# Joint first query blocks, four score banks with one visit per pair, an all-fp32r second batch and a lower VectorE bias in a planned attention + gated-MoE kernel

## The chip, the cores and the metric

One core of a Trainium2 chip runs the whole program. The metric is device time in microseconds; three runs of the kernel before gave 697.58, 698.43 and 699.06, median 698.43. Engines are called PE (TensorE matmul), PEld (its weight loads), DVE (VectorE), ACT (ScalarE), POOL (GpSimd) and SP (the queue that issues the DMAs). L443 is line 443 of the kernel.

## The reference: what is computed

```python
batch, n_heads, seq, head_dim = (4, 12, 448, 64)
scores = scale * np.matmul(q, k.transpose(0, 1, 3, 2))
scores = np.where(mask, -1000000000.0, scores)          # causal
scores = scores - np.max(scores, axis=-1, keepdims=True)
attn = np.exp(scores)
attn = attn / (np.sum(attn, axis=-1, keepdims=True) + 1e-09)
attn_out = np.matmul(attn, v)
# heads side by side: 1792 tokens x 768, then the gated feed-forward, d_ff = 1536
g = x @ w_gate
silu = g * (1.0 / (1.0 + np.exp(-g)))
out = silu * (x @ w_val) @ w_out
```

All of it is float32, causal attention over 4 batches of 12 heads, then three matrix products over 1792 tokens.

## The kernel before, in words

**Tiling.** The 448 queries of a batch are one chunk (`CHUNKS`), and the chunk is also the token tile of the feed-forward. Heads are worked in pairs (6 pairs per batch, 24 in all), the even head's operands on partitions 0 to 63 and the odd one's on 64 to 127, so that the two heads' score matmuls stand side by side in the array. Queries are cut at 0, 64, 192, 320, 448: block 0 has 64 queries, the others 128. Block i needs the keys up to its own end, so the scores of one head are 64, 192, 320 and 448 wide.

**Attention, per pair.** Scores (L443) go to PSUM banks `S`; DVE adds the causal mask, takes the row maximum and writes to SBUF (L467, `p`); ACT takes exp with the row sums (L478); DVE makes the reciprocal of the sums (L489, L490); the rows are scaled (norm: L499 on ACT, L503 on POOL, or a DVE form); PE transposes the result into PSUM banks `T` in three groups per head, group 0 shared by the two heads (L548, 4 transposes), groups 1 and 2 of 3 transposes each for either head (L577); the `T` bank is copied out (`ph`, L293); then PE multiplies with V into bank `O` (PV) and the result goes to `xs`.

**Two arithmetics.** `NS` and `NP` say by batch how scores and PV are done. `n` is plain float32 (L443 on `qraw`, `kraw`; L640). `s` splits each operand into two fp32r parts, hi and lo, and makes three fp32r passes for the scores (L443 on `QS`, `KS`) and two for PV (L612 with `ph`, L614 with `pl`; block 0 in one pass, hi and lo stacked). There `ph` is the hi part, made by ACT, and DVE makes the lo part from the same `T` bank (L315), so the bank is free only after both. In batch 0 all six pairs are `n`, in batch 1 the even pairs, in batches 2 and 3 none: 9 pairs `n`, 15 pairs `s`.

**Feed-forward.** Weights come as 36 groups of 128 x 768. In chunk 0 each group is put together from raw 64-bit words (`wide`, `top`, `wraw`), split into hi and lo (`whl`) and stored for the later chunks, which load it. A group needs 18 matmuls of 448 columns (L742 to L744, three fp32r passes, banks `M`): 2592 in all. The planner places them in units of three.

**Order.** Nothing is issued in the order of the code. Each step is an `op` with a due time, dependencies, the buffers it takes and frees, and a cost on each engine that can do it. `Planner.run` gives every engine its list, in which the engines then run strictly; `BIAS` is added to an engine's finishing time when alternatives are compared, `LAT` stands for the time from one engine to another, and `CAPS` says how many buffers a tag has. PSUM has 8 banks: `S` 2, `T` 3, `O` 1, `M` 2. The scores of a pair are two ops: blocks 0 and 3 in one visit of PE, blocks 1 and 2 in another (`SG`), each with one `S` bank per head (in batch 0 the second takes `M`).

Of the kernel before, what the change touches and what calls it, by code (L numbers as in the profile page):

```python
# [8 lines left out]
F32 = mybir.dt.float32  # L9
# [8 lines left out]
P = 128  # L18
D = 64
# [9 lines left out]
UW = 0  # L29
NS = ['n', 'ns', 's', 's']  # L30
NP = ['n', 'ns', 's', 's']
LEN = [46.6, 112.0, 258.9, 133.6, 58.1]
# [17 lines left out]
DLAT = 1.8  # L50
CAPS = {'S': 2, 'T': 3, 'O': 1, 'M': 2, 'qraw': 3, 'kraw': 3, 'vraw': 3, 'QS': 1, 'KS': 1, 'VS': 3, 'ph': 2, 'pl': 2, 'p': 2, 'tmp': 2, 't': 3, 'osb': 2, 'wide': 3, 'wraw': 2, 'whl': 5}

# [168 lines left out]
def kernel(  # L221
# [34 lines left out]
    back, mask = masks[:, : maskX + P], masks[:, P:]  # L256
    sums = [cpool.tile([P, NKC], F32, tag=f"sums{i}", name=f"sums{i}") for i in range(NR)]
    rec = [cpool.tile([P, NKC], F32, tag=f"rec{i}", name=f"rec{i}") for i in range(NR)]
    xs = [cpool.tile([P, T], F32, tag=f"xs{i}", name=f"xs{i}") for i in range(KD)]
# [6 lines left out]
    nc.vector.memset(top, 0)  # L266
    for t_ in sums:
        nc.vector.memset(t_, 1.0)
    make_identity(nc, ident)
    nc.gpsimd.memset(masks, 0.0)  # L270
    for m_, step, base in ((back, 1, 1 - P), (mask, -1, maskX)):
        nc.gpsimd.affine_select(
            out=m_, in_=m_, pattern=[[step, maskX + P]], compare_op=ALU.is_ge,
            fill=BIG, base=base, channel_multiplier=1,
        )

    pl_ = Planner()
# [81 lines left out]
    st = [dict() for _ in range(NU)]  # L359
    loads, scored, parts = {}, {}, {}  # L360
    ptile, pfirst, normed, first0, dues = {}, {}, {}, {}, {}
    xs_ops, xs_res, xlast = {}, {}, {}

    def attention(u):
# [8 lines left out]
        if h % 2 == 0:  # L373
# [24 lines left out]
        if not npv:  # L398
            rV = Res("VS")

            def newv():
# [4 lines left out]
                           lambda: raw(s["VS"])[:, :, 0:D]), due(9), [v1], [], [rV, rv])  # L406

        rsum = Res(f"sums{u % NR}")
        exps, rps = [], {}
        if h % 2 == 0:  # L410
            if not U.ns:
                rQ, rK = Res("QS"), Res("KS")
                sp = []
                for nm, r_, src, ld, rr in (("Q", rQ, "q", lq, rq), ("K", rK, "k", lk, rk)):
                    def newsp(nm=nm):
# [4 lines left out]
                                        lambda nm=nm: raw(s[nm])[:, 0]), due(1), [x1], [], [r_, rr]))  # L420
            for gi_, sess in enumerate(SG):
                stag = "M" if c == 0 and gi_ % 2 else "S"
                rSs = {(y, x): Res(stag) for y in (0, 1) for x in range(len(sess))}

                def score(gi_=gi_, sess=sess, stag=stag):
                    passes = ((None, None),) if U.ns else ((0, 0), (0, 1), (1, 0))
                    for x, blks in enumerate(sess):
                        B_ = [bank(stag, f"S{u + y}_{gi_}_{x}") for y in (0, 1)]
                        off = 0
                        for i in blks:  # L430
                            q0, q1_ = U.qi[i][1]
                            for y in (0, 1):
                                st[u + y][f"S{i}"] = B_[y][:, off : off + q1_]
                            off += q1_
                    for x, blks in enumerate(sess):
                        for i in blks:
                            q0, q1_ = U.qi[i][1]
                            for z, (a, b_) in enumerate(passes):
                                for y in (0, 1):
                                    half = slice(D * y, D * y + D)  # L440
                                    Q = s["qw"][half] if U.ns else s["Q"][half, a]
                                    K = s["kw"][half] if U.ns else s["K"][half, b_]
                                    nc.tensor.matmul(st[u + y][f"S{i}"][: U.rows[i]], Q[:, q0 : q0 + U.rows[i]], K[:, :q1_] if y else K[:, S - q1_ :],  # L443
                                                     start=z == 0, stop=z == len(passes) - 1)
                ws = [U.qi[i][1][1] for blks in sess for i in blks]
                if U.ns:
                    so = op({"PE": (sum(cost("PE", "n", w) + 0.06 for w in ws) + TS, score), "kind": "s"}, due(2), [lq, lk],
                            list(rSs.values()), [rq, rk])
# [7 lines left out]
        for i, (q0, q1_) in U.qi:  # L456
            r = U.rows[i]
            sl = U.pslot(q1_)
            rp = ptile[u, i] if h % 2 else Res(f"p{sl}")
            so, rS = scored[u, i]  # L460

            def rowmax(i=i, q0=q0, q1_=q1_, r=r, sl=sl):
                if h % 2 == 0:
                    s[f"pp{i}"] = st[u + 1][f"pp{i}"] = buf([P, 2 * q1_], F32, f"p{sl}", "p", f"p{u}_{i}")
                p = s[f"p{i}"] = s[f"pp{i}"][:, (h % 2) * q1_ : (h % 2 + 1) * q1_]
                m = s[f"m{i}"] = pool.tile([P, 1], F32, tag=f"m{sl}", name=f"m{u}_{i}", bufs=2 * CAPS["p"])
                nc.vector.tensor_tensor_reduce(  # L467
# [8 lines left out]
            def expo(i=i, r=r):  # L476
                p = s[f"p{i}"]
                nc.scalar.activation(  # L478
                    p[:r], p[:r], AF.Exp, bias=s[f"m{i}"][:r], scale=-1.0,
                    accum_out=sums[u % NR][:r, i : i + 1],  # L480
# [5 lines left out]
        def recip():  # L486
            i0, i1 = U.qi[0][0], U.qi[-1][0] + 1
            sm, rc = sums[u % NR][:, i0:i1], rec[u % NR][:, i0:i1]
# [4 lines left out]
        norms = {}  # L493
        for i, (q0, n) in U.qi:
            r = U.rows[i]

            def na(i=i, r=r):
# [13 lines left out]
            }, due(6), [rc], [], [rps[i], rsum])  # L511

        blocks = parts[u] = {}
        normed[u] = norms
# [23 lines left out]
        if h % 2:  # L538

            rT = Res("T")  # L540
            both_ = [norms[i] for i in norms] + [normed[u - 1][i] for i in norms]

            def transp0():
                pt = s["T0"] = st[u - 1]["T0"] = bank("T", f"T{u}_0")
                for i, (q0, _) in U.qi:
                    r = U.rows[i]
                    w = U.qi[i][1][1]
                    nc.tensor.transpose(pt[:, q0 : q0 + r], s[f"pp{i}"][:r, w - D : w + D], ident[:r, :r])  # L548
            tr = op({"PE": (0.109 * len(U.qi), transp0), "kind": "t"}, due(7), both_, [rT], list(rps.values()))
            if npv:  # L550
                rh = Res("ph0")

                def newp():
                    s["ph0"] = st[u - 1]["ph0"] = buf([P, N], F32, "ph0", "ph", f"ph{u}_0")
                    return s["ph0"]
                hi = op(copies("psum", N, newp, lambda: s["T0"][:, :N], engines="AD"), due(8), [tr], [rh], [rT])
                for y in (0, 1):
# [7 lines left out]
        for g, js in enumerate([[1], [2, 3]], 1):  # L565
            cols = [U.qb - U.base(j) for j in js]
            offs = [sum(cols[:i]) for i in range(len(js))]
            n = sum(cols)
            rT = Res("T")
            todo = [(j, o_, i, e) for j, o_ in zip(js, offs) for i, e in U.qi if e[0] >= U.kb[j][0]]  # L570

            def transp(g=g, todo=todo):
                pt = s[f"T{g}"] = bank("T", f"T{u}_{g}")
                for j, o_, i, (q0, q1_) in todo:
# [21 lines left out]
    def weigh(u):  # L596
# [33 lines left out]
        for j in range(nj):  # L630
# [3 lines left out]
            def pv(g=g, j=j, o_=o_, w=w):  # L634
                if j == 0:
                    st[u0]["O"] = bank("O", f"O{u}")
                for v in (u0, u):
                    half = D * (v - u0)
                    kr = parts[v][j][3]
                    nc.tensor.matmul(st[u0]["O"][half : half + D, U.base(j) - U.qa : N], st[v]["v"][kr, j],  # L640
                                     st[v][f"ph{g}"][kr, o_ : o_ + w], start=(j == 0), stop=(j == nj - 1))
            dur = cost("PE", "n", w) + 0.02
            last = op({"PE": (dur + (TV if j == 0 else 0), pv), "kind": "v"}, due(10), d0 + d1 + [last],
# [240 lines left out]
```

## Time and profile before

| what | value |
|---|---|
| median of 3 runs | 698.43 us (697.58 to 699.06) |
| the profiled execution: its time, its span | 697.08 us, 695.3 us |
| PE busy | 682.3 us, 98% of the span |
| PEld, DVE, ACT, POOL busy | 598.1, 333.8, 346.9, 162.6 us |
| granted clock of PE, whole span | 1.0 of full speed |
| DMA | 165.05 MB, 236 GB/s on HBM over the span |
| PE rows of the feed-forward (L742 to L744) | 2592 |

A matmul's row is longer than its turn: matmuls are pipelined, and the next starts before the row ends. What a matmul costs is therefore read from starts: within a stream of M matmuls they are 0.20 us apart. "A visit" below is a stretch of PE's list with one kind of work (scores, transposes, PV) between two stretches of M matmuls. Its cost is taken as the time from the last M's start before it to the third M's start after it, less three times 0.20. A float32 matmul is recorded as two rows, so that x8 in such a row is four instructions.

### The profile page before, as it was taken

The numbers are of one execution on the slowest core, as the hardware profiler recorded it, in microseconds if no ns is written. First come the engines' busy times: TensorE is split into PE (matmuls) and PEld (weight loads), VectorE is DVE, ScalarE is ACT, GpSimd is POOL, SyncE is SP. The second block draws the span as 40 slices with busy tenths as digits, with TensorE's granted clock in tenths as the row PEclk, the third lists the DMA queues.
The fourth block names the chain that finished last, engine by engine and source line by source line (L and its number), as shares of the span: only waits on it lengthen the run. The fifth ranks groups of instructions, "written<-read, shape, count | busy, mean of one in ns | idle before, by whom it ended". The sixth has DMA issues, their size and how long they took to land.

```text
span 695.3 us, 10644 instructions
## 1 busy us (share of the span) xinstructions
PE 682.3 (98%) x3834; PEld 598.1 (86%) x3834; DVE 333.8 (48%) x851; ACT 346.9 (50%) x882; POOL 162.6 (23%) x212
## 2 busy tenths in 40 slices
PE   7899999999999999999999999999999999999997
PEld 4467898888889889889889898988988999999997
DVE  5877877589473544555533255455544212222100
ACT  6999666578683644554634356255455311111000
POOL 3756234145121331222312113122131000000000
PEclk9999999999999999999999999999999999999999
DMA  8994999978989656546567665545555576666771
GB/s 325 292 339 154 366 419 380 332 277 310 384 309 326 209 182 197 206 178 204 187 218 228 206 210 197 187 152 179 183 163 182 183 236 226 222 210 214 234 250 40
DMA packets 39796, 165.05 MB, mean 237 GB/s; under 512 B 4416, under 2 KB 13632, under 8 KB 39744
## 3 DMA queue, kind: packets, MB, share of 16 engines
q1 hardware_dynamic: 39744, 164.38, 67.9%
q8 instruction: 30, 0.49, 0.3%
q14 instruction: 22, 0.18, 0.1%
HBM read 130.55 MB, written 33.82 MB: 236 GB/s over the span
## 4 chain that ended last, share of the span: by engine, by line
PE 89%; ACT 6%; DVE 2%; issue 0%; DMA 0%; POOL 0%; SPq 0%; ACTq 0%; POOLq 0%
PE M L742 16%; PE M L743 15%; PE M L744 15%; PE MO L742 9%; PE MO L743 8%; PE MO L744 8%; PE S L443 6%; PE T L577 4%; PE O L612 3%; ACT p L499 2%; PE O L640 2%; ACT p L478 2%; PE O L614 2%; ACT ph L293 1%; PE T L548 1%; DVE p L467 1%
## 5 line engine op out<-in xcount | busy, mean ns | idle before, releaser
L742 PE MATMUL M<-xh,whl 128*128 128x448 f32 x576 | 215.6, 374 | 0.0
L743 PE MATMUL M<-xl,whl 128*128 128x448 f32 x576 | 209.3, 363 | 0.0
L744 PE MATMUL M<-xh,whl 128*128 128x448 f32 x576 | 209.0, 363 | 0.0
L742 PEld LDWEIGHTS M<-xh,whl 128*128 128x128 f32 x576 | 108.2, 188 | 15.2 <-issue 8.5
L478 ACT ACTIVATE p<-p,m 128x64 f32<-128x64 f32 (+3 forms) x192 | 96.3, 511 | 38.3 <-DVE m L467 36.9
L744 PEld LDWEIGHTS M<-xh,whl 128*128 128x128 f32 x576 | 108.0, 188 | 7.7
L743 PEld LDWEIGHTS M<-xl,whl 128*128 128x128 f32 x576 | 108.4, 188 | 6.5
L742 PE MATMUL MO<-hh,whl 128*128 128x448 f32 x288 | 107.2, 372 | 0.0
L743 PE MATMUL MO<-hl,whl 128*128 128x448 f32 x288 | 104.7, 363 | 0.0
L744 PE MATMUL MO<-hh,whl 128*128 128x448 f32 x288 | 104.5, 363 | 0.0
L467 DVE CUSTOM_DVE_ANT_0 p<-S,masks 128x64 f32<-128x64 f32 (+1 forms) x192 | 70.2, 419 | 53.6 <-PE S L443 51.0
L293 ACT ACTIVATE ph<-T 128x384 fp32r<-128x384 f32 (+3 forms) x133 | 60.9, 507 | 38.3 <-PE T L548 23.1
L293 ACT ACTIVATE hh<-t 128x448 fp32r<-128x448 f32 x41 | 23.6, 575 | 76.6 <-DVE t L784 76.6
L742 PEld LDWEIGHTS MO<-hh,whl 128*128 128x128 f32 x288 | 54.1, 188 | 6.0 <-issue 2.5
L499 ACT ACTIVATE p<-p,rec 128x192 f32<-128x192 f32 (+3 forms) x132 | 57.0, 504 | 3.0 <-DVE rec L489 1.7
L784 DVE TENSOR_TENSOR t<-t,M 128x448 f32<-128x448 f32 x48 | 29.7, 620 | 58.6 <-PE M L744 58.4
L778 DVE SCALAR_TENSOR_TENSOR t<-t,M 128x448 f32<-128x448 f32 x48 | 29.7, 620 | 58.6 <-ACT t L774 57.9
L744 PEld LDWEIGHTS MO<-hh,whl 128*128 128x128 f32 x288 | 54.0, 188 | 3.9
L743 PEld LDWEIGHTS MO<-hl,whl 128*128 128x128 f32 x288 | 54.2, 188 | 3.4
L774 ACT ACTIVATE t<-M 128x448 f32<-128x448 f32 x48 | 26.0, 541 | 54.3 <-PE M L744 53.8
L293 ACT ACTIVATE osb<-MO 128x448 f32<-128x448 f32 x24 | 13.0, 544 | 64.9 <-PE MO L744 64.6
L503 POOL TENSOR_SCALAR p<-p,rec 128x320 f32<-128x320 f32 (+3 forms) x60 | 34.4, 584 | 46.8 <-ACT p L478 21.9
(61 smaller groups left out, 800.7 us busy)
## 6 DMA issues: line engine op xcount, KB each, us to landing
whl<-ws SPq DMA_DIRECT2D x108, 768.0 KB, 4.3
wide<-in_w_dram SPq DMA_DIRECT2D x36, 768.0 KB, 7.0
ws<-whl SPq DMA_DIRECT2D x36, 768.0 KB, 6.5
vraw<-in_v_dram SPq DMA_DIRECT2D x24, 256.0 KB, 4.7
qraw<-in_q_dram SPq DMA_DIRECT2D x24, 224.0 KB, 4.8
kraw<-in_k_dram SPq DMA_DIRECT2D x24, 224.0 KB, 4.9
out_dram<-osb SPq DMA_DIRECT2D x24, 224.0 KB, 4.7
```

What stands on the lines that cost most here:

```text
L293: nc.scalar.activation(out(), in_(), AF.Copy, scale=scale)
L443: nc.tensor.matmul(st[u + y][f"S{i}"][: U.rows[i]], Q[:, q0 : q0 + U.rows[i]], K[:, :q1_] if y else K[:, S - q1_ :], start=z == 0, stop=z ...
L467: nc.vector.tensor_tensor_reduce(p[:r], s[f"S{i}"][:r], mask[:r, maskX - q0 : maskX - q0 + q1_] if h % 2 else back[:r, P - min(q1_, P) : P ...
L478: nc.scalar.activation(p[:r], p[:r], AF.Exp, bias=s[f"m{i}"][:r], scale=-1.0, accum_out=sums[u % NR][:r, i : i + 1],)
L499: nc.scalar.activation(p[:r], p[:r], AF.Copy, scale=rec[u % NR][:r, i : i + 1])
L503: nc.gpsimd.tensor_scalar(p[:r], p[:r], rec[u % NR][:r, i : i + 1], 0.0, ALU.mult, ALU.add)
L577: nc.tensor.transpose(pt[:, o_ + q0 - bs : o_ + q0 - bs + r], s[f"p{i}"][:r, k0 : k0 + P], ident[:r, :r])
L742: nc.tensor.matmul(out[:, :n], a[:, w], xhi, start=first, stop=False)
L743: nc.tensor.matmul(out[:, :n], a[:, w], xlo, start=False, stop=False)
L744: nc.tensor.matmul(out[:, :n], l[:, w], xhi, start=False, stop=last)
L778: nc.vector.scalar_tensor_tensor(t, t, 1.0, ps[c, f, 0][:, :N], ALU.add, ALU.mult)
L784: nc.vector.tensor_tensor(t, t, ps[c, f, 1][:, :N], ALU.mult)
```

## The change

1. `NS`, `NP`: batch 1 is all `s`; `n` remains for the six pairs of batch 0.
2. In a batch-0 pair the two heads' first query blocks (64 queries each) become one tile of 128 partitions: two 64x64 score matmuls into one bank, one row maximum, one exp, one norm (which writes its output interleaved, 128x64x2), one transpose. Before, each head had its own 64-wide block of 128 rows. The copy out of `T` group 0 is then 512 wide in place of 448, and PV's first block is done in two pieces (64 and 384 columns).
3. From batch 1 on the four score blocks of a pair are one op, in ascending order, with four banks (`S` 2, `X` 2). `T` has one bank there; in batch 0 the `T` groups take turns over two `X` banks and the `T` bank.
4. `BIAS` of DVE falls from 1.3 to 0.8, that of ACT and POOL.
5. Small: sums and reciprocals are slices of one tile each, the maxima of a head columns of one tile; one memset replaces eight.

```diff
-NS = ['n', 'ns', 's', 's']
-NP = ['n', 'ns', 's', 's']
+NS = ['n', 's', 's', 's']
+NP = ['n', 's', 's', 's']
...
-BIAS = {'DVE': 1.3, 'ACT': 0.8, 'POOL': 0.8}
+BIAS = {'DVE': 0.8, 'ACT': 0.8, 'POOL': 0.8}
...
-CAPS = {'S': 2, 'T': 3, 'O': 1, 'M': 2,
...
+CAPS = {'S': 2, 'X': 2, 'T': 1, 'O': 1, 'M': 2,
...
+            self.joint = self.ns and self.np
+            self.own = [(i, e) for i, e in self.qi if i or h % 2 == 0 or not self.joint]
...
+    def ttag(c):
+        turns[0] += 1
+        return "T" if c or turns[0] % 3 == 0 else "X"
...
-            for gi_, sess in enumerate(SG):
-                stag = "M" if c == 0 and gi_ % 2 else "S"
-                rSs = {(y, x): Res(stag) for y in (0, 1) for x in range(len(sess))}
+            for gi_, sess in enumerate(SG if c == 0 else [sum(SG, [])]):
+                tags = ["S", "X"] if c else ["MS"[gi_ == 0]]
+                rSs = {(y, x): Res(tags[x]) for x in range(len(sess)) for y in (0, 1)}
+                steps = sorted(sum(sess, []))
...
+                                if U.joint and i == 0:
+                                    nc.tensor.matmul(st[u]["S0"][half], Q[:, :D], K[:, :D] if y else K[:, S - D :], start=True, stop=True)
+                                    continue
...
+                    nc.vector.tensor_tensor_reduce(p[:, D:], s["S0"], both, -0.125, 3.0e38, ALU.add, ALU.min, m)
...
+                    nc.scalar.activation(p, p, AF.Exp, bias=peak(0), scale=-1.0, accum_out=sums[u % NR][:, 0:1])
...
+                    t = s["pp0"]
+                    return (t.rearrange("p (a b) -> p b a", a=2), t[:, D:].unsqueeze(2).broadcast_to([P, D, 2]), rec[u % NR][:, 0:1])
...
+                        o = pt.rearrange("p (a b) -> p a b", b=D)[:, :: N // D]
+                        nc.tensor.transpose(o, s["pp0"], ident)
...
-            rT = Res("T")
+            rT = Res(ttag(c))
...
+                cuts = ((q0, D, N), (D, N - D, D)) if U.joint and j == 0 else ((q0, w, o_),)
```

Three places of the engines' lists show what moves. The first is PE's list in batch 2, where the scores of one pair end a visit and the next begins (S_0 and S_1 are the two score ops of before; M is the feed-forward; the last number is the width). Before:

```order
L443 MATMUL S_0_0_3027<-KS_2796,QS_2794 128x448
L443 MATMUL S_0_0_3028<-KS_2796,QS_2794 128x448
L742 MATMUL M_6_3020<-xh_91,whl_2855 128x448
L743 MATMUL M_6_3020<-xl_97,whl_2855 128x448
L744 MATMUL M_6_3020<-xh_91,whl_2855 128x448
L742 MATMUL M_6_3020<-xh_92,whl_2855 128x448
L743 MATMUL M_6_3020<-xl_98,whl_2855 128x448
L744 MATMUL M_6_3020<-xh_92,whl_2855 128x448
```

In the changed kernel's list, at a pair of batch 2 (S_0_0 is a bank of tag `S`, S_0_1 one of tag `X`):

```order
L463 MATMUL S_0_0_3929<-KS_3684,QS_3682 128x64
L463 MATMUL S_0_0_3930<-KS_3684,QS_3682 128x64
L463 MATMUL S_0_1_3931<-KS_3684,QS_3682 128x192
L463 MATMUL S_0_1_3932<-KS_3684,QS_3682 128x192
L463 MATMUL S_0_1_3931<-KS_3684,QS_3682 128x192
L463 MATMUL S_0_1_3932<-KS_3684,QS_3682 128x192
L463 MATMUL S_0_1_3931<-KS_3684,QS_3682 128x192
L463 MATMUL S_0_1_3932<-KS_3684,QS_3682 128x192
L463 MATMUL S_0_1_3931<-KS_3684,QS_3682 128x320
```

The M matmuls that stood between the two visits of a pair are gone from there: 24 score matmuls follow each other. Over the list the fp32r score visits go from 30 (15 pairs) to 18 (18 pairs).

The second is the transposes of a pair's odd head, on PE too (T_0, T_1, T_2 are the three groups; O is PV of the even head). Before, in batch 2:

```order
L548 MATMUL T_0_3496<-ident,p_3_3332 128x128
L577 MATMUL T_1_3501<-ident,p_1_3375 128x128
L577 MATMUL T_1_3501<-ident,p_2_3382 128x128
L577 MATMUL T_1_3501<-ident,p_3_3332 128x128
L577 MATMUL T_2_3507<-ident,p_2_3382 128x128
L577 MATMUL T_2_3507<-ident,p_3_3332 128x128 x2
L742 MATMUL M_15_3481<-xh_93,whl_3297 128x448
```

In the changed kernel:

```order
L612 MATMUL T_0_3820<-ident,p_3_3692 128x128
L812 MATMUL M_21_3812<-xh_78,whl_3624 128x448
L813 MATMUL M_21_3812<-xl_84,whl_3624 128x448
L814 MATMUL M_21_3812<-xh_78,whl_3624 128x448
L812 MATMUL M_21_3812<-xh_79,whl_3624 128x448
L813 MATMUL M_21_3812<-xl_85,whl_3624 128x448
L814 MATMUL M_21_3812<-xh_79,whl_3624 128x448
L812 MATMUL M_21_3812<-xh_80,whl_3624 128x448
L813 MATMUL M_21_3812<-xl_86,whl_3624 128x448
L814 MATMUL M_21_3812<-xh_80,whl_3624 128x448
L677 MATMUL O_3841<-ph_0_3829,VS_3347 128x448
```

With one bank, T_1 can't follow T_0 at once: nine M matmuls stand behind T_0, then PV of the even head, then T_1. A pair's five transpose groups are five visits where they were two. Of the 18 fp32r pairs 14 have exactly nine M's between T_0 and PV, three have twelve and one fifteen.

The third is DVE's list early in batch 0, around the first reciprocal (p_1 to p_3 are the scores of blocks 1 to 3 on their way to probabilities; the rows m 128x1 belong to the row maxima). Before:

```order
L489 TENSOR_SCALAR rec_76<-sums_68 128x4
L490 RECIPROCAL rec_76<-rec_76 128x4
L467 ISA p_3_305,m_3_306<-S_0_0_277,masks 128x448
L467 ISA m_3_306 128x1
L467 ISA p_0_292,m_0_310<-S_0_0_278,masks 128x64
```

In the changed kernel:

```order
L524 TENSOR_SCALAR rec<-sums 128x4
L525 RECIPROCAL rec<-rec 128x4
L502 ISA p_3_279,m_267<-S_0_0_254,masks 128x448
L502 ISA m_267 128x1
L565 TENSOR_SCALAR p_2_260<-p_2_260,rec 128x320
L565 TENSOR_SCALAR p_3_242<-p_3_242,rec 128x448
```

Norms (L565) stand on DVE, where there was none. In all DVE gets 88 norms and 78 other SBUF-to-SBUF copies of one input (hh 28, VS 22, top 11, whl 9, xh 8); ACT's rows of the list fall from 692 to 589, POOL's from 216 to 131.

## Rows read from the trace of the kernel before

**Rows 1.** Timeline of PE, start and length in us: the first M matmul.

```profile
43.71 0.45 PE L742 MATMUL M<-xh,whl 128*128 128x448 f32 x1
```

**Rows 2.** Waits: engine, line, whom it waited for: us, times, longest.

```profile
PEld O L612 <- DVE ph L315: 4.3, 12, 0.4
...
PE S L443 <- DMA kraw<-in_k_dram: 4.0, 1, 4.0
```

**Rows 3.** Windows: length, busy us (x instructions) by engine, clock, DMA share, GB/s.

```profile
17.00:47.00 30.00, 26.02 (x182) 15.22 (x181) 24.50 (x85) 30.00 (x99) 22.76 (x26) 1.00 0.93 322
...
60.00:200.00 140.00, 139.89 (x789) 120.26 (x788) 101.85 (x203) 99.56 (x222) 49.79 (x46) 1.00 0.88 332
200.00:550.00 350.00, 349.82 (x2005) 313.50 (x2004) 164.21 (x442) 173.08 (x450) 77.79 (x118) 1.00 0.60 200
```

**Rows 4.** Timeline of PE: the two score visits of an fp32r pair.

```profile
333.02 0.36 PE L744 MATMUL M<-xh,whl 128*128 128x448 f32 x1
333.31 1.22 PE L443 MATMUL S<-KS,QS 64*128 64x64 f32 x12
334.46 0.47 PE L742 MATMUL M<-xh,whl 128*128 128x448 f32 x1
334.77 0.37 PE L743 MATMUL M<-xl,whl 128*128 128x448 f32 x1
334.97 0.36 PE L744 MATMUL M<-xh,whl 128*128 128x448 f32 x1
...
337.06 1.04 PE L443 MATMUL S<-KS,QS 64*128 64x192 f32 x12
...
338.56 0.37 PE L744 MATMUL MO<-hh,whl 128*128 128x448 f32 x1
```

**Rows 5.** Timeline of PE: a transpose visit of two groups, and the third M behind.

```profile
342.97 0.82 PE L577 MATMUL T<-ident,p 128*128 128x128 f32 x6
...
344.04 0.36 PE L744 MATMUL MO<-hh,whl 128*128 128x448 f32 x1
```

**Rows 6.** Timeline of PE: an fp32r PV visit without a wait.

```profile
243.66 0.54 PE L612 MATMUL O<-ph,VS 128*128 128x448 f32 x2
244.04 0.34 PE L614 MATMUL O<-pl,VS 128*128 128x384 f32 x1
...
245.08 0.36 PE L744 MATMUL M<-xh,whl 128*128 128x448 f32 x1
```

**Rows 7.** Timeline of PE: one score visit and the PV visit of float32 pairs.

```profile
45.70 1.25 PE L443 MATMUL S<-kraw,qraw 64*128 64x64 f32 x8
46.87 0.47 PE L742 MATMUL M<-xh,whl 128*128 128x448 f32 x1
...
81.25 2.42 PE L640 MATMUL O<-ph,vraw 64*64 64x448 f32 x16
83.59 0.47 PE L742 MATMUL M<-xh,whl 128*128 128x448 f32 x1
```

**Rows 8.** Timeline, all engines: from transpose group 0 to the PV that waits for it.

```profile
294.81 0.60 PE L548 MATMUL T<-ident,p 128*128 128x128 f32 x4
...
295.45 1.99 ACT L293 ACTIVATE ph<-T 64x448 fp32r<-64x448 f32 x4 [1.69 <-PE T L548]
...
296.57 1.28 DVE L315 TENSOR_TENSOR ph<-T,ph 64x448 fp32r<-64x448 f32 x2 [2.17 <-ACT ph L293]
...
296.92 0.36 PE L744 MATMUL M<-xh,whl 128*128 128x448 f32 x1
297.25 0.65 PE L612 MATMUL O<-ph,VS 128*128 128x448 f32 x2
297.73 0.34 PE L614 MATMUL O<-pl,VS 128*128 128x384 f32 x1
```

**Rows 9.** Timeline of DVE: the same small operation beside a POOL operation, and alone.

```profile
230.02 0.93 DVE L489 TENSOR_SCALAR rec<-sums 128x4 f32<-128x4 f32 x1
...
231.08 0.14 DVE L489 TENSOR_SCALAR rec<-sums 128x4 f32<-128x4 f32 x1
```

More of the change, by code (lines that the diff above doesn't have):

```diff
@@ L266 @@
     nc.vector.memset(top, 0)
-    for t_ in sums:
-        nc.vector.memset(t_, 1.0)
+    nc.vector.memset(all_sums, 1.0)
     make_identity(nc, ident)
@@ L435, in score @@
[L435 to L444, printed above, removed]
@@ L446, in attention @@
+                ws = [U.qi[i][1][1] for i in steps]
                 if U.ns:
-                    so = op({"PE": (sum(cost("PE", "n", w) + 0.06 for w in ws) + TS, score), "kind": "s"}, due(2), [lq, lk],
-                            list(rSs.values()), [rq, rk])
+                    so = op({"PE": (sum(cost("PE", "n", w) + 0.06 for w in ws) + TS, score), "kind": "s"}, due(2),
+                            [lq, lk], list(rSs.values()), [rq, rk])
                 else:
@@ L493, in attention, with views, na0, npl0 @@
         norms = {}
-        for i, (q0, n) in U.qi:
+        for i, (q0, n) in U.own:
             r = U.rows[i]
+            if U.joint and i == 0:
+                def views():
+                    t = s["pp0"]
+                    return (t.rearrange("p (a b) -> p b a", a=2), t[:, D:].unsqueeze(2).broadcast_to([P, D, 2]), rec[u % NR][:, 0:1])
+                def na0():
+                    o, a, m = views()
+                    nc.scalar.activation(o, a, AF.Copy, scale=m)
+                def npl0():
+                    o, a, m = views()
+                    nc.gpsimd.tensor_scalar(o, a, m, 0.0, ALU.mult, ALU.add)
+                def nd0():
+                    o, a, m = views()
+                    nc.vector.tensor_scalar(o, a, m, None, ALU.mult)
+                norms[0] = op({
+                    "ACT": (cost("ACT", "ptr", P), na0), "POOL": (cost("POOL", "ptr", P), npl0),
+                    "DVE": (cost("DVE", "one", P), nd0), "port": True,
+                }, due(6), [rc], [], [rps[0], rsum])
+                continue
             def na(i=i, r=r):
@@ L538, in attention, with transp0 @@
         if h % 2:
-            rT = Res("T")
-            both_ = [norms[i] for i in norms] + [normed[u - 1][i] for i in norms]
-            def transp0():
-                pt = s["T0"] = st[u - 1]["T0"] = bank("T", f"T{u}_0")
+            rT = Res(ttag(c))
+            both_ = [norms[i] for i in norms] + [normed[u - 1][i] for i in normed[u - 1]]
+            def transp0(rT=rT):
+                pt = s["T0"] = st[u - 1]["T0"] = bank(rT.tag, f"T{u}_0")
                 for i, (q0, _) in U.qi:
@@ L636, in pv @@
                     st[u0]["O"] = bank("O", f"O{u}")
[L637 to L642, printed above, removed]
+                q0 = U.base(j) - U.qa
+                cuts = ((q0, D, N), (D, N - D, D)) if U.joint and j == 0 else ((q0, w, o_),)
+                for q_, n, r_ in cuts:
+                    for v in (u0, u):
+                        half = D * (v - u0)
+                        kr = parts[v][j][3]
+                        a = r_ if half else q_ - q0 + o_
+                        nc.tensor.matmul(st[u0]["O"][half : half + D, q_ : q_ + n], st[v]["v"][kr, j],
+                                         st[v][f"ph{g}"][kr, a : a + n], start=j == 0 and q_ == 0, stop=j == nj - 1)
+            dur = cost("PE", "n", w) + (0.15 if U.joint and j == 0 else 0.02)
             last = op({"PE": (dur + (TV if j == 0 else 0), pv), "kind": "v"}, due(10), d0 + d1 + [last],
```

79 lines of the change are left out of this document (56 added, 23 removed).

## The prediction

> **What bounds the kernel now.** I read the windows first [rows 3]. [...] So past the start nothing but PE's own list counts: whatever shortens it shows one to one, and another engine matters only where it makes PE wait. Before that it is ACT: between 17 and 47 us it has no idle time at all, and PE has gaps. Then the waits [rows 2]. Two lines matter: 4.0 us until the first k lands, which no edit here touches, and 4.3 us in 12 waits of PV's weight load for DVE's lo part. Last I took single visits from the timeline [rows 4 to 7]. PE runs so evenly (0.20 us per M, the same in every stretch) that a visit's price can be read from starts.
>
> The profiled execution took 697.08 us: span 695.3, 1.8 around it. The sum is made against it. The median of the three runs lies 1.35 us above, which I add at the end.
>
> **Prices of visits.** They go by the definition in the section on the profile. Where a first row is missing, the last M stands 0.29 us before a score or float32 PV visit (333.02 to 333.31) and 0.20 before any other.
> - Scores, fp32r, two visits: 334.97 - 333.02 - 0.60 = 1.35, and (338.56 - 337.06) + 0.29 - 0.60 = 1.19. A pair: 2.54 us [rows 4].
> - Transposes: 344.04 - 342.97 + 0.20 - 0.60 = 0.67 for six, 0.11 each; a visit as such adds 0.01 to 0.02 [rows 5].
> - PV, fp32r, no wait: 245.08 - 243.66 + 0.20 - 0.60 = 1.02 per head, 2.04 per pair [rows 6].
> - Float32: the row before M's first gives scores (46.87 - 45.70) + 0.09 in front + 0.11 behind = 1.37 for half a pair, 2.7 per pair; PV (83.59 - 81.25) + 0.20 = 2.54 per pair [rows 7]. The 0.11 is 334.77 - 334.46, less 0.20 [rows 4].
>
> **The change part by part.**
>
> *One score visit in place of two (15 pairs that were fp32r already).* Of a visit, 0.09 in front and 0.11 behind are seen as longer starts, so at least 0.20 goes per pair. What the 24 matmuls carry, two side by side, is 3 x 1024 columns at 0.20 per 448 = 1.37 us, and some 0.3 for the narrow ones (0.11 is what a 128-wide transpose takes, and I take it as the least turn for 64 and 192 columns); so 2.54 holds about 0.86 of overhead, 0.43 per visit, the upper bound. I take 0.35, nearer the upper end since the starts of only the outer rows are in the 0.20: 15 x 0.35 = **-5.3** (-3.0 to -6.5).
>
> *Five transpose visits in place of two.* The same 16 transposes; three more visits of 0.01 to 0.02: 18 x 0.04 = **+0.6**. M matmuls fill between, and they have to be done anyway.
>
> *Three pairs from float32 to fp32r.* 2.7 + 2.54 = 5.2 falls to (2.54 - 0.35) + 2.04 = 4.2: 3 x 1.0 = **-3.0** (-2.6 to -3.3). The splits of Q, K and V and the lo parts that they add lie on DVE, ACT and POOL, whose cover in 60 to 200 us is about 27% of idle time [rows 3]; what it costs if that cover is gone is the first rival below.
>
> *The waits at transpose group 0.* [Rows 8] show the chain: T0 starts at 294.81, ACT's first copy at 295.45, DVE's first lo part only at 296.57, after ACT's second copy (two of 0.55), and PV at 297.25. From T0's start to PV 2.44 us. In the changed list nine M's stand between. T0's four transposes and nine M's take 0.36 (0.58 for six, less two of 0.11; the first M at 343.55) + 0.28 + 0.21 + 7 x 0.20 + 0.01 = 2.26, so PV waits about 0.18, and its second matmul comes 0.10 late as well (297.73 - 297.25 = 0.48 against 0.38 in [rows 6]), because the next weight load is not ahead: 0.28 to 0.30 each. At 14 places: **+4.1**. Where twelve or fifteen M's stand, none. What goes is the 12 waits of before: 4.3 / 12 = 0.36 in place of the usual 0.20, and 0.10 behind, 0.26 each: **-3.1**. Net **+1.0** (-3 to +2).
>
> *The single T bank otherwise.* A pair hands the bank on four times at short distance, 72 times in all. The chain of a 384-wide group: 0.20 from the last transpose to ACT, 0.5 and 0.6 for the two copies; 1.3 us. Nine M's give 1.8. So with ACT and DVE at hand nothing waits, with 0.5 us in hand. An engine that is at that moment in a longer operation costs up to 0.5 without effect and then one to one. I take **+1.5** (0 to +10; the top end is the rival).
>
> *The joint first block.* Two mode changes more per pair (64x64 tiles beside 64x128 ones, PV in two pieces). The nearest row is a visit's lead-in, 0.09 [rows 4]: 6 x 0.1 = **+0.6** (0 to +1.2). Its gain lies on the other engines.
>
> *The start.* PE's list ahead of its first M (43.71 us, [rows 1]) held 6 pairs of scores, 70 transposes and 4 pairs of PV: 16.2 + 7.7 + 10.2 = 34 us of work, so about 9.6 us of waits, of which 4.0 for the first DMA. The rest, 5.6, waited for ACT. In batch 0 ACT made 116 activations and 51 reads of the sums; now 84 and 42. At 30.0 / 99 = 0.30 us per instruction [rows 3] that is 12 us of some 50 less, or 8.4 us per pair becoming 6.4, against 5.8 to 5.9 of PE. In exchange DVE gets 22 norms and a few copies. No row of before shows such a norm: below, the small operation of 0.14 us [rows 9], above, the 64x448 lo part at 0.64 [rows 8]. I take 0.35, halfway: 8 us on DVE, which in 17 to 47 us had 5.5 of 30 idle, or some 10 over the whole of batch 0 (50 us of ACT). So all three engines end near 6 us per pair, and of the 5.6 us about half should go: **-2.5** (-5.6 to +3: if DVE now sets the pace, or too few M's are ready to fill).
>
> What the norm costs bears on this only. [...]
>
> Sum: -5.3 + 0.6 - 3.0 + 1.0 + 1.5 + 0.6 - 2.5 = **-7.1**. 697.1 - 7.1 = 690.0 for an execution like the profiled one, 691.3 as median; I say **691.5**, with its own range 687 to 696.
>
> **Rivals.**
>
> *DVE becomes late and the single T bank hands it to PE (slower).* One mechanism: with three banks a lo part that came a microsecond late cost nothing; with one, the next transposes wait for it, and PE runs in order, so all M's behind stand too. For it: DVE takes 88 norms and 78 copies on top, at 73% already up to 200 us, and it can be held up: the same 128x4 operation took 0.93 us beside a POOL operation and 0.14 alone [rows 9]. Against it: POOL's list shrinks by two fifths, nine to fifteen M's cover 1.8 to 3.0 us, and after 200 us DVE has half its time free. Price: a hold-up of 0.8 less the 0.5 in hand, and 0.1 behind, is 0.4; if half of the 72 hand-overs meet one and the rest small ones, 18 us in place of my 1.5: 691.3 + 16.5 = **708**. It decides from a mean of 0.12 us over all 72 on (8.6 us, where the gain of 7.1 is used up). [...]
>
> *Gain and loss cancel.* The start gains nothing, because DVE replaces ACT as its bound (22 norms at 0.64 make 14 us), and the hand-overs cost 6: -7.1 + 2.5 + 4.5 = 0, **698**. For it: all three engines come out near 6 us per pair in the start. Against it: PE's list is shorter whatever they do.
>
> *All of it comes.* Score visits at the upper bound, no waits at group 0 because DVE takes its lo part earlier, the whole 5.6 of the start: -6.5 + 0.6 - 3.3 - 3.0 + 0.3 - 5.6 = -17.5; with a part of these, -12 to -17, about **684**. For it: PE never waited past the start for anything but [rows 2]'s 12 waits, so the plan's distances have held so far.
>
> **How the numbers follow.** Forecast 0.60, slower by late DVE 0.14, cancelling 0.13, all of it 0.13. The least that a measurement tells from no change is 0.2%, 1.4 us. Faster: 0.60 + 0.13 = 0.73; same 0.13; slower 0.14. The range must leave out 2 in 10: below 685.5 only the better half of the last case lies (0.07), above 699.5 most of the slower one (0.12). So 685.5 to 699.5.
>
> **What would show it right or wrong.** Right: M matmuls still 0.20 apart; fp32r score visits of x24 at 2.1 to 2.3 us; PV behind T0 starting 0.3 to 0.4 after the last M at about 14 places; transposes of groups 1 and 2 without gaps in front; the first M near 42 us although more work stands ahead of it; DVE norms of 448 columns at 0.3 to 0.4. Wrong: gaps of PE in front of T1 and T2 waiting for DVE's pl, above all at 60 to 200 us with DVE over 90% busy; norms of 0.6 us or many of 0.8 to 1.2 beside POOL; a start in which PE waits for DVE; score visits of x24 at 2.5 us, by which the largest term would be gone.

## The result, and the profile after

The changed kernel takes 704.18 us (median, 702.96 to 706.04) beside 698.56 us before (697.30 to 699.33): 5.6 us slower, ratio 1.0089, 95% interval 1.0075 to 1.0103. Forecast was 691.5 us.

The profiled execution took 703.47 us, span 701.7. Its windows; the first runs from 10 to 44 us where [rows 3] have 17 to 47, and the last is not in [rows 3] (length, busy us and instructions of each engine, clock, DMA share, GB/s):

```profile
10.00:44.00 34.00, 31.91 (x221) 17.75 (x217) 33.66 (x116) 30.99 (x99) 15.21 (x17) 0.95 0.81 276
60.00:200.00 140.00, 139.47 (x805) 125.11 (x805) 129.48 (x277) 97.75 (x223) 35.74 (x40) 1.00 0.94 349
200.00:550.00 350.00, 348.50 (x1989) 311.76 (x1988) 198.19 (x557) 145.12 (x388) 44.45 (x53) 1.00 0.61 203
600.00:650.00 50.00, 50.00 (x244) 45.48 (x243) 15.21 (x27) 3.59 (x7) 0.00 (x0) 1.00 0.63 215
```

The same last stretch, and the start, in the kernel before:

```profile
10.00:44.00 34.00, 29.05 (x204) 16.73 (x201) 27.56 (x106) 34.00 (x113) 24.00 (x29) 1.00 0.95 336
600.00:650.00 50.00, 50.00 (x251) 46.92 (x251) 12.75 (x21) 7.88 (x14) 0.00 (x0) 1.00 0.67 219
```

The last row of each is the finding. From 600 to 650 us no attention is left, PE does nothing but M matmuls of one shape at a granted clock of 1.00 in both, and DVE and ACT are mostly idle. Before does 251 of them in 50 us, the changed kernel 244. Nothing in the diff touches them.

PE's timeline of the changed kernel, around one score visit (start, length):

```profile
334.26 0.37 PE L812 MATMUL M<-xh,whl 128*128 128x448 f32 x1
334.47 0.37 PE L813 MATMUL M<-xl,whl 128*128 128x448 f32 x1
334.67 0.37 PE L814 MATMUL M<-xh,whl 128*128 128x448 f32 x1
334.97 1.99 PE L463 MATMUL S<-KS,QS 64*128 64x64 f32 x24
336.89 0.47 PE L812 MATMUL M<-xh,whl 128*128 128x448 f32 x1
...
337.40 0.36 PE L814 MATMUL M<-xh,whl 128*128 128x448 f32 x1
337.60 0.37 PE L812 MATMUL M<-xh,whl 128*128 128x448 f32 x1
337.81 0.37 PE L813 MATMUL M<-xl,whl 128*128 128x448 f32 x1
338.01 0.37 PE L814 MATMUL M<-xh,whl 128*128 128x448 f32 x1
```

The x24 visit costs (337.40 - 334.67) - 0.60 = 2.13 us, within the forecast 2.1 to 2.3 [rows 4]. But the M's are 0.20 and 0.21 apart in turn: to the nanosecond 207, 207, 206.

The whole difference can be booked by charging each PE row from its start to the next one's. The first M came at 45.19 us in place of 43.71 [rows 1]. After it, all visits other than M fell from 112.3 to 106.8 us: -5.5. The 2592 M's rose from 535.2 to 545.6: +10.4. Together 1.5 - 5.5 + 10.4 = +6.4, the distance of the two profiled executions. "Steady M's" below are those from the fourth of a stretch on (2166 before, 2127 after): a mean distance of 200.6 ns before, 206.1 after.

The kernel before had shown that a second distance exists. Its timeline behind one transpose visit:

```profile
512.99 0.45 PE L742 MATMUL MO<-hh,whl 128*128 128x448 f32 x1
...
513.48 0.36 PE L744 MATMUL MO<-hh,whl 128*128 128x448 f32 x1
513.68 0.37 PE L742 MATMUL MO<-hh,whl 128*128 128x448 f32 x1
513.89 0.37 PE L743 MATMUL MO<-hl,whl 128*128 128x448 f32 x1
514.10 0.37 PE L744 MATMUL MO<-hh,whl 128*128 128x448 f32 x1
514.30 0.37 PE L742 MATMUL MO<-hh,whl 128*128 128x448 f32 x1
```

From 513.68 to the next visit 207 ns, then 200 again. 189 of its M's stand in such stretches.

### The profile page after: what moved, and what is told of

Read it like the earlier page. It is cut to its first block, busy times and chain, and to the rows that moved or that the text cites. A ratio compares the mean times of both kernels' runs of the same rounds, so it can differ in the third digit from the quotient of the medians.

```text
span 701.7 us, 10719 instructions
## 1 busy us (share of the span) xinstructions
PE 689.7 (98%) x3876; PEld 603.7 (86%) x3876; DVE 412.7 (59%) x1063; ACT 304.1 (43%) x773; POOL 103.3 (15%) x128
## 4 chain that ended last, share of the span: by engine, by line
PE 89%; DVE 8%; ACT 1%; issue 0%; DMA 0%; SPq 0%; ACTq 0%
PE M L812 16%; PE M L813 16%; PE M L814 16%; PE MO L812 8%; PE MO L813 8%; PE MO L814 8%; PE S L463 6%; PE T L642 4%; PE O L677 3%; DVE p L502 2%; PE O L679 2%; DVE p L565 2%; PE T L612 1%; DVE wraw L795 1%; PE O L710 1%; DVE whl L319 0%
## 5 line engine op out<-in xcount | busy, mean ns | idle before, releaser
L812 PE MATMUL M<-xh,whl 128*128 128x448 f32 x576 | 217.9, 378 | 0.0
L813 PE MATMUL M<-xl,whl 128*128 128x448 f32 x576 | 211.9, 368 | 0.0
L814 PE MATMUL M<-xh,whl 128*128 128x448 f32 x576 | 211.9, 368 | 0.0
L812 PE MATMUL MO<-hh,whl 128*128 128x448 f32 x288 | 108.5, 377 | 0.0
L297 ACT ACTIVATE ph<-T 64x448 fp32r<-64x448 f32 (+2 forms) x130 | 64.8, 504 | 96.8 <-PE T L612 53.5
L814 PE MATMUL MO<-hh,whl 128*128 128x448 f32 x288 | 105.9, 368 | 0.0
L513 ACT ACTIVATE p<-p,m 128x192 f32<-128x192 f32 (+3 forms) x180 | 91.1, 508 | 7.7 <-DVE m L502 7.6
L502 DVE CUSTOM_DVE_ANT_0 p<-S,masks 128x192 f32<-128x192 f32 (+3 forms) x180 | 68.6, 430 | 21.1 <-PE S L463 20.9
L319 DVE TENSOR_TENSOR pl<-T,ph 128x384 fp32r<-128x384 f32 x72 | 39.6, 550 | 28.6 <-ACT ph L297 28.4
L319 DVE TENSOR_TENSOR ph<-T,ph 64x448 fp32r<-64x448 f32 x36 | 22.4, 622 | 50.4 <-ACT ph L297 49.8
L642 PE MATMUL T<-ident,p 128*128 128x128 f32 x288 | 47.9, 278 | 1.4 <-DVE rec L524 0.5
L642 PEld LDWEIGHTS T<-ident,p 128*128 128x128 f32 x288 | 34.1, 141 | 13.0 <-issue 3.0
```

The lines of the kernel that those rows point to most:

```text
L297: nc.scalar.activation(out(), in_(), AF.Copy, scale=scale)
L319: r["DVE"] = (cost("DVE", "two", n), lambda: nc.vector.tensor_tensor(out(), a(), b(), alu))
L502: nc.vector.tensor_tensor_reduce(p[:r], s[f"S{i}"][:r], mask[:r, maskX - q0 : maskX - q0 + q1_] if h % 2 else back[:r, P - min(q1_, P) : P ...
L513: nc.scalar.activation(p[:r], p[:r], AF.Exp, bias=peak(i)[:r], scale=-1.0, accum_out=sums[u % NR][:r, i : i + 1],)
L642: nc.tensor.transpose(pt[:, o_ + q0 - bs : o_ + q0 - bs + r], s[f"p{i}"][:r, k0 : k0 + P], ident[:r, :r])
L812: nc.tensor.matmul(out[:, :n], a[:, w], xhi, start=first, stop=False)
```

## The experiments

The matmul itself, its operands' shapes and PSUM banks (2 and 3) are the same in both kernels. What moved is memory: the sums and reciprocals became one tile each, `both` came in, `m` became one tile per head, `ph0` of the odd head grew. The streamed tiles xh, xl, hh, hl kept their addresses (xh0 at byte 30592 of a partition), the weight tiles whl went from 166368 to 166496.

### Address or order of visits

All with every instruction in its place. **e1**, the changed kernel:

```diff
-                s["m"] = pool.tile([P, NKC], F32, tag="m", ...
+                s["m"] = mpool.tile([P, NKC], F32, tag="m", ...
```

> The changed kernel, every instruction in its place; only the four small tiles m (128 bytes a partition in all) are put behind the other tiles, so that the weight tiles whl stand again at the address that they had in the kernel before (166368 in place of 166496). Address theory (where whl stands decides whether one M matmul follows the last by 200 or by 207 ns): the median M to M distance is 200 ns again, some 2474 x 7 ns = 17 us come back, and the time is 684 to 690 us. Order theory (the distance is left behind by the visits that come between the M groups: 3 and 4 transposes, 4 PV, 24 scores in place of 6 and 10, 7, 12): 206 to 207 ns stays, 702 to 706 us. Company theory (VectorE's and the DMA's work beside it): 206 to 207 ns stays as well.

**e2**, the kernel before, and **e4**, e1 with the same two lines and 16 in place of 32:

```diff
         def newhl():
+            if i == 0:
+                pool.tile([P, 32], F32, tag="pad", name="pad")
```

> The kernel before, every instruction in its place, with an unused 128 bytes a partition set aside ahead of the first weight tile, so that whl and what is set aside after it stand 128 bytes on, whl at 166496 as in the changed kernel. Address theory: most M to M distances go from 200 to 206 or 207 ns, and the time from 698.6 to 712 to 717 us. Order theory and company theory: 200 ns and 698 to 699 us stay.

**e3** sets the same tile aside in `newsp`, where QS is first made.

> The kernel before with the same 128 bytes set aside behind the weight tiles: whl stays at 166368, and only QS, KS, VS, t, pl, tmp and osb stand 128 bytes on. If whl's own address decides: 200 ns and 698 to 699 us stay. If the address of one of the other tiles decides (through the visits between the M groups): 206 to 207 ns and 712 to 717 us as in the run with all of them moved.

> The changed kernel with m behind the other tiles and 64 bytes set aside ahead of whl, which then stands at 166432, halfway between the two places. Address theory: the distance may be 200, 206 to 207, or a mixture; 200 (684 to 690 us) would say that the step lies in the second 64 bytes, 207 (702 to 706 us) in the first. Order theory and company theory: 206 to 207 ns and 702 to 706 us in any case.

Measured: e1 698.73 us (ratio 1.0005, 0.9994 to 1.0015), e2 706.09 (1.0112, 1.0097 to 1.0127), e3 697.97, e4 702.23. Steady M's 203.1, 204.0, 201.0 and 205.3 ns. Moving whl and what stands behind it made the old kernel 8 us slower, and taking it back gave the new one 5.5 us; moving only what stands behind it did nothing. So whl's address is a cause. (e1 moves p, ph and wraw back as well; e2 and e3 together are the clean pair.) The stretch from 600 to 650 us in e2, then in e3:

```profile
600.00:650.00 50.00, 50.00 (x246) 45.79 (x245) 12.88 (x21) 7.34 (x13) 0.00 (x0) 1.00 0.66 217
```

```profile
600.00:650.00 50.00, 50.00 (x252) 46.92 (x251) 13.08 (x21) 7.50 (x15) 0.00 (x0) 1.00 0.66 220
```

But neither theory holds pure: e1 came back to 200 ns only in part. There 16 of the 18 stretches behind a visit of 4 transposes run at 207 and 17 of 18 behind PV with 3 transposes at 200. The place fixes which distances there are. What picks one of them for a stretch stays open: it is not the kind of visit ahead alone, since in e10 below, with the same list and the same distance between the operands, 6 of 18 run at 207 behind either visit.

The company theory is out, since neither move changes what runs beside. The end of the program says the same. In the changed kernel the last weights land at 683.7 us, and from then on DVE and POOL are idle and ACT nearly so; the M's still come at 206.7 ns. 12 us there, and 12 us about as far from the end of e8, the run below at 200.0 ns:

```profile
685.00:697.00 12.00, 12.00 (x59) 10.91 (x59) 0.00 (x0) 0.55 (x1) 0.00 (x0) 1.00 0.08 28
```

```profile
673.00:685.00 12.00, 12.00 (x62) 11.25 (x61) 0.00 (x0) 0.55 (x1) 0.00 (x0) 1.00 0.11 40
```

### Which place

**e5**, **e6**, **e7**, **e8** (e7's kernel, timed) and **e9**: the same two lines with 8 (whl at 166400) or 24 (166464) in place of 32, in the changed kernel with `mpool` (e5, e7, e8) and in the one before (e6, e9).

> The changed kernel, every instruction in its place, m behind the other tiles and 32 bytes set aside ahead of whl, so that the weight tiles begin at 166400, a whole number of 64-byte and of 512-byte steps, where every place tried so far (166368, 166432, 166496) lies 32 bytes off a 64-byte step. Step theory (rows of weights that begin in the middle of a 64-byte step are what costs): every M to M distance is 200 ns or less and the same after every visit, 684 to 690 us. Phase theory (address and visits together choose among several repeating patterns, and no place is free of it): a mixture of 200, 205 and 207 ns as in the three places so far, 696 to 704 us.

> The kernel before with 32 bytes set aside ahead of whl, so that it begins at 166400. Step theory: M to M 200 ns or less throughout; the kernel before had 189 of some 2590 M matmuls in stretches of 207 ns, which makes 1 to 2 us, so 696 to 698 us. Phase theory: more stretches of 205 and 207 ns than the kernel before has, 699 to 708 us.

> The changed kernel with whl at 166464, a whole number of 64-byte steps but 64 bytes off a 512-byte step. Step theory with 64 bytes: as at 166400, 684 to 690 us and 200 ns throughout. If only the whole 512 bytes count: a mixture, 696 to 704 us. Phase theory: a mixture here and at 166400.

> The kernel of the single look that gave 690.77 us (the changed kernel, whl at 166464), timed in rounds against the kernel before. If the M distance of about 200 ns there belongs to the place: 690 to 692 us, ratio 0.988 to 0.992. If it was the luck of one execution: 696 to 704 us.

> The kernel before with 96 bytes set aside ahead of whl, so that it begins at 166464 as in the run of 690.77 us. It gives what the change is worth when both kernels have their weights at the same, good place. Place theory: every M distance within 197 to 201 ns, 695 to 698.5 us, so the change is worth 5 to 7 us. Phase theory (the visits of each kernel decide as much as the place): stretches of 203 to 207 ns come in here, 700 to 706 us.

**e10** moves the streamed tiles along with the weights:

```diff
+    pad = cpool.tile([P, 16], F32, tag="pad", name="pad")
     xs = [cpool.tile([P, T], F32, tag=f"xs{i}", name=f"xs{i}") for i in range(KD)]
```

> The changed kernel with m behind the other tiles and 64 bytes set aside ahead of xs, so that the streamed tiles xh, xl, hh and hl and the weight tiles all stand 64 bytes on: xh at 30656, whl at 166432. If the distance between the weights and the streamed tiles decides, it is that of the run with whl at 166368 and xh at 30592: stretches of 200 and of 207 ns, 697 to 699 us. If whl's own place decides, it is as with whl at 166432 and xh at 30592: 202 to 209 ns in one pattern with a mean of 205, 701 to 703 us. Something else: the place of both counts.

**e12**, **e13**, **e14**: the changed kernel without `mpool` and with 8, 16 and 24, which makes the grid of 32 bytes complete.

> The changed kernel with 32 bytes set aside ahead of whl, which stands at 166528. The streamed tiles stand 1792 = 7 x 256 bytes apart and the weight blocks 512 apart, so all pairs of a weight block and a streamed tile have one distance modulo 256: whl less xh0 (30592), here 0. So far: 96 gave stretches of 200 and 206.7 ns (697.7 to 698.9 us in two placements), 128 gave 204 (699), 160 gave 205.3 (702), 192 gave 200.0 in two orders of the visits (691.9), 224 gave 206.1 (704). Place theory: one mean here too, and the time lies on the line 691.9 + 2.59 x (mean M distance - 200.0 ns), within 1.5 us. Theory that 192 is the one good place: 203 to 207 ns, 699 to 710 us. Theory that the visits decide: 206 ns as in the changed kernel, 704 us.

> The changed kernel with 64 bytes set aside ahead of whl (166560; distance 32 modulo 256). Place theory: a mean of its own, the time on the line 691.9 + 2.59 x (mean - 200.0) within 1.5 us. Theory that 192 is the one good place: 203 to 207 ns, 699 to 710 us. Theory that the visits decide: 206 ns, 704 us.

> The changed kernel with 96 bytes set aside ahead of whl (166592; distance 64 modulo 256), the last of the eight places on the 32-byte grid. Place theory: a mean of its own, the time on the line 691.9 + 2.59 x (mean - 200.0) within 1.5 us. Theory that 192 is the one good place: 203 to 207 ns, 699 to 710 us. If the period is 128 bytes, this is as 192: 200.0 ns, 691.9 us.

Measured (distance: whl less xh0, modulo 256; one execution where no ratio is given):

| distance | whl at | changed kernel: us, ratio | steady M, ns | kernel before: us, ratio | steady M, ns |
|---|---|---|---|---|---|
| 0 | 166528 | 700.21 | 204.4 | | |
| 32 | 166560 | 699.19 | 203.6 | | |
| 64 | 166592 | 695.47 | 202.3 | | |
| 96 | 166368 | 698.73, 1.0005 (e10: 698.90) | 203.1 (e10: 203.7) | 698.56, 1 | 200.6 |
| 128 | 166400 | 699.17, 1.0027 | 203.9 | 703.44, 1.0086 | 203.9 |
| 160 | 166432 | 702.23 | 205.3 | | |
| 192 | 166464 | 691.91, 0.9917 (0.9903 to 0.9930) | 200.0 | 696.47, 0.9985 (0.9976 to 0.9993) | 199.9 |
| 224 | 166496 | 704.18, 1.0089 | 206.1 | 706.09, 1.0112 | 204.0 |

The step theory fell: 166400, a multiple of 512, is no better than most. The distance between weights and streamed tiles decides, not whl's own address: e10, with both moved, has whl where e4 had it, but e1's two distances, 200 and 207 ns, where e4 has a run of 202 to 209 (e10 and e4 are one execution each). At 192 both orders of visits give the same. My line through the mean missed e12 to e14 by 2.1 to 3.0 us: I had charged all 2592 M's, though the ones just behind a visit don't follow it. With the 2127 steady ones it holds within 1.2 us at every place. Why these distances, the runs don't show; that stays open.

The last stretch at distance 192 (e8), and at 64 (e14):

```profile
600.00:650.00 50.00, 50.00 (x252) 46.87 (x251) 15.05 (x27) 3.27 (x6) 0.00 (x0) 1.00 0.66 220
```

```profile
600.00:650.00 50.00, 50.00 (x249) 46.35 (x249) 15.44 (x28) 3.28 (x6) 0.00 (x0) 1.00 0.63 221
```

252, 249, and 244 in the changed kernel as it came: the same work in the same 50 us.

### The terms, with the weights at 166464

**e11** and **e16** put the scores of a pair in two visits again:

```diff
-            for gi_, sess in enumerate(SG if c == 0 else [sum(SG, [])]):
-                tags = ["S", "X"] if c else ["MS"[gi_ == 0]]
+            for gi_, sess in enumerate(SG):
+                tags = ["SX"[gi_]] if c else ["MS"[gi_ == 0]]
...
-                    so = op({"PE": (sum(3 * cost("PE", "r", w) ..., "kind": "s"}, due(2), sp,
+                    so = op({"PE": (sum(3 * cost("PE", "r", w) ..., "kind": "s"}, due(2 + 2 * gi_), sp,
```

e11 has the first two lines, e16 all three.

> The changed kernel with whl at 166464 and the scores of a pair of heads in the later batches in two visits of 12 matmuls again, each with its two banks of the four. My term: 15 visits more at 0.35 us, 5.3 us more than with one visit, so 695 to 697 us. Rival: a visit costs little when its banks are free, since the M matmuls only move aside, so 690 to 692 us.

> The changed kernel with whl at 166464 and the scores of an fp32r pair in two visits of 12, as in the earlier run with two visits, but the second one due 2 us later, since there the planner put the two visits of nearly every pair next to each other. Now M matmuls stand between them in all 18 pairs. My term: 18 x 0.35 = 6.3 us more than the 691.9 of one visit, 697 to 699 us (from the single visits of the two kernels with whl at 166464, 2 x 1.26 against 2.12: 18 x 0.40 = 7.2). Rival: the overhead of a visit is smaller than that, 692 to 695 us.

Measured: e11 694.55 us (0.9956, 0.9943 to 0.9968), which tells little: the planner put the two visits side by side in 15 of 18 pairs. e16, all 18 apart: 702.41 (1.0066, 1.0051 to 1.0081), 10.5 us more than e8. In the nine pairs of which both visits stand alone they cost 2.53 us together, in place of 2.12: 18 x 0.41 = 7.4, which bears out the 7.2 from single visits and is somewhat more than my term of 6.3. Of the other 3 us, 1 is a later start in the profiled execution (first M 46.42; traces of one and the same list differ by up to 2 us there), and 1 is waits of PE past the start, 3.5 us in e16 and 2.4 in e8; the rest is not accounted for. The longest in e16's list behind the first load's (engine, line, whom it waited for: us, times, longest; 1.6 of the first row stands in the start, as in e8):

```profile
PE T L643 <- DVE p L566: 2.8, 3, 1.6
PE O L678 <- DVE ph L320: 2.1, 1, 2.1
```

**e17** sets `NS` and `NP` of the second batch back to `'ns'`.

> The changed kernel with whl at 166464 and the second batch as in the kernel before, three of its six pairs in float32 (here with the joint first block). My term: three pairs at 1.0 us, 3.0 us more, 694.5 to 695.5 us; the joint block's pieces may add 0.3. Rival: float32 pairs cost PE more but need no splits and no lo parts, and VectorE is over 90% busy there, so the two cancel: 691 to 693 us.

Measured: 691.48 us (0.9917, 0.9902 to 0.9931), not to be told from e8. The rival holds: three pairs in fp32r are worth nothing here. It holds by its own reason too: past the start PE waited 0.9 us in e17 and 2.4 in e8.

**e15** and **e18** change one number:

```diff
-BIAS = {'DVE': 0.8, 'ACT': 0.8, 'POOL': 0.8}
+BIAS = {'DVE': 1.3, 'ACT': 0.8, 'POOL': 0.8}
```

e18 has 1.0.

> The changed kernel with whl at 166464, and the planner's surcharge for VectorE at 1.3 again in place of 0.8, so that fewer norms and copies go to VectorE. Theory that VectorE holds up the start (in the run of 691.91 us it was busy 33.6 of 34 us from 10 to 44 us, and PE waited 2.7 us there for its norms): the start gets 1 to 3 us shorter, 688.5 to 691 us. Rival: ScalarE takes over as the bound and nothing is won, 691 to 694 us. The M distance stays 200.0 ns by both.

> The changed kernel with whl at 166464 and the planner's surcharge for VectorE at 1.0, between the 1.3 of before (690.8 us) and the 0.8 of the change (691.9). If the start's bound moves smoothly from VectorE to ScalarE: 689 to 691 us, the best of the three. If the plan's order jumps with any number: 690 to 693 us.

Measured: e15 690.82 us (0.9895, 0.9878 to 0.9911), e18 688.84 (0.9870, 0.9854 to 0.9887), the best of all and better than both kernels. The start in e8, then in e18:

```profile
10.00:44.00 34.00, 30.53 (x225) 17.30 (x223) 33.54 (x118) 31.18 (x100) 15.19 (x17) 1.00 0.77 272
```

```profile
10.00:44.00 34.00, 31.65 (x231) 18.91 (x228) 32.22 (x115) 32.70 (x103) 16.74 (x21) 1.00 0.86 302
```

In the kernel before ACT (the fourth number behind the length) had no idle time at all, in e8 DVE has 0.5 us of 34, in e18 both have over 1. The first M stands at 45.37 us in e8 and here in e18:

```profile
42.62 0.47 PE L815 MATMUL M<-xh,whl 128*128 128x448 f32 x1
```

e15 starts earlier still (42.03) and gives it back in four later gaps of PE of over 0.5 us, the longest at 59.35 us, from where the next M comes 1.49 us later; so the order of the plan counts beside the load.

## Why the prediction was wrong

**The step that failed** is the first sign of its last part, "M matmuls still 0.20 apart", and the sentence it rests on, that PE needs "0.20 us per M, the same in every stretch". The sum has no term for M. Measured: +10.4 us, more than all the gains, and the cause is whl's place, 128 bytes on: that move alone made the kernel before 8 us slower (e2). None of the three rivals had it. The sentence was also wrong of the kernel before: 189 of its M's stand in stretches at 207 ns. The mean over a stretch hides that; the starts row by row show it.

**What the rest was worth.** With the weights at 166464 the changed kernel takes 691.9 us, against a forecast of 691.5. Against the kernel before at the same place it is 0.9917 / 0.9985, or 4.6 us (696.47 - 691.91), where the sum said 7.1. That 691.9 lies so near 691.5 is luck: the good place gives the kernel before some 1 us too, and several terms were off against each other. Term by term, e9 and e8 beside the forecast:

- One score visit, -5.3: a pair fell from 2 x 1.27 to 2.12 us in seven of the eight x24 visits that stand alone (the eighth waited: 3.71), so 15 x 0.41 = -6.2, or -4.6 with that wait. Right.
- Five transpose visits, +0.6: 0.69 + 1.10 = 1.79 before, 0.45 + 4 x 0.338 = 1.80 after. 0.0. (18 x 0.04 is 0.7; the sum has 0.6.)
- Three pairs to fp32r, -3.0: beside the kernel before, 5.2 us fell to 4.4, so -2.4. But for the edit by itself, nothing (e17). Its price for float32 was that of the old float32 pair; with one score visit and the joint block such a pair costs 4.6, and e17's shorter waits make up for the rest.
- Group 0, net +1.0: the mechanism right, the net nothing: PV of a pair as a whole cost 2.28 us before and 2.26 after. Its chain as in [rows 8]:

```profile
323.49 0.60 PE L612 MATMUL T<-ident,p 128*128 128x128 f32 x4
...
324.12 1.09 ACT L297 ACTIVATE ph<-T 64x448 fp32r<-64x448 f32 x2 [0.51 <-PE T L612]
...
325.25 1.27 DVE L319 TENSOR_TENSOR ph<-T,ph 64x448 fp32r<-64x448 f32 x2 [0.99 <-ACT ph L297]
...
325.57 0.37 PE L814 MATMUL M<-xh,whl 128*128 128x448 f32 x1
325.92 0.30 PEld L677 LDWEIGHTS O<-ph,VS 128*128 128x128 f32 x2 [0.36 <-DVE ph L319]
325.92 0.65 PE L677 MATMUL O<-ph,VS 128*128 128x448 f32 x2
...
326.40 0.34 PE L679 MATMUL O<-pl,VS 128*128 128x384 f32 x1
```

  From T0 to PV 2.43 us (forecast 2.44), PV 0.35 after the last M (0.3 to 0.4), its second matmul 0.48 later (0.48). In the list of waits 13 such places where the forecast had 14, beside [rows 2]:

```profile
PEld O L677 <- DVE ph L319: 4.9, 13, 0.4
```

- The single T bank, +1.5: about right in size. And the late-DVE rival: 36 visits of three transposes stand alone; beyond 36 x 0.338 they took 1.2 us in the changed kernel and 2.2 in e8. So PE lost little at transposes, though DVE is busy 92% from 60 to 200 us. The one longer wait past the start is at a score visit that comes 7 us behind the last one, before DVE has read out its four banks. In all of the changed kernel's list of PE's waits, behind the first load's:

```profile
PE T L612 <- DVE p L565: 1.4, 1, 1.4
PE S L463 <- DVE m L502: 1.2, 1, 1.2
PE T L642 <- DVE rec L524: 0.5, 1, 0.5
PE T L642 <- ACT p L557: 0.2, 1, 0.2
PE T L642 <- DVE ph L319: 0.2, 1, 0.2
```

  The mechanism was possible, but it is not what made the kernel slower. That rival's 708 lay near the measured time by coincidence.
- The joint block and the start, +0.6 and -2.5: wrong in sign. Until batch 0's last PV ends, PE's time without M's (0.20 each) and without batch 1's scores was 51.7 us before and 52.5 after: +0.8. DVE took over from ACT as the bound, as the second rival said of the start; e8's PE stood 1.14 and 1.64 us there for DVE's norms (PE's timeline; the granted clock is 0.95 in the changed kernel from 10 to 44 us and 1.00 in e8, whose first M is no earlier, so the clock is not it; in all traces with 1.00 up to 44 us that time is 51.6 to 51.7 us in four of the list before and 52.1 to 52.7 in three of the changed list):

```profile
13.75 0.99 PE L613 MATMUL T<-ident,p 128*128 128x128 f32 x3 [1.14 <-DVE p L566]
...
19.58 0.66 PE L643 MATMUL T<-ident,p 128*128 128x128 f32 x4 [1.64 <-DVE p L566]
```

  In the changed kernel a norm of 448 columns took 0.448 us in the median of 32, not my 0.35. With less on DVE (e18) part of the gain came: e18's first M is 2.75 us ahead of e8's, and until batch 0's last PV it took 51.0 us.

Added up, -6.2 + 1.6 - 2.4 + 2.2 + 1.0 (the start from e9 to e8, 51.7 to 52.7) = -3.8 of the 4.6 measured; the rest is not accounted for.

## What to carry to other kernels

Before trusting a sum of visits, check that the matmuls nobody touched will keep their pace: a change that adds or resizes a tile moves every tile allocated behind it, and here 32 bytes were worth 12 us. Print the addresses of both builds; where matmuls alone fill a stretch, count them per window; and time a small change only against a kernel with its operands at an equally good place, or it measures the place. A planner's weights want a second pass once the layout is settled: the best kernel here differs from the changed one in a place and one number.

## What the runs showed of the hardware

The same 128x448 matmul with the same 128x128 weight load, back to back at a granted clock of 1.00 (600 to 650 us in the changed kernel and in the one before), follows at a mean of 199.9 ns (e9) to 206.1 ns (the changed kernel), depending on where the weights stand relative to the streamed operand. Single distances of steady M's go from 199 to 208 ns in the traces of the kernel before and the changed one, in fixed patterns: behind the last visit 206, 207, 207 over and over in the changed kernel. At one place two patterns exist (in the kernel before 200, and 207 in the stretches of those 189 M's), and a stretch keeps the one that it has settled in, longest behind the last visit: 200.0 ns from 556 to 691 us in the kernel before, 206.7 from 561 to 698 us in the changed one.

The place matters: 706.09 us (e2) against 697.47 for one kernel, with nothing but whl and what stands behind it moved by 128 bytes, and 697.97 (e3) when only the latter moved. What in the chip makes it so was not tried.
